# Down products in longer runs: the order of TensorE's work in stage three of a spectral and gated feed-forward kernel

## The chip, the cores and the metric

One core of a Trainium2 chip runs the whole program. The metric is the time on the device in microseconds (us); lower is better. TensorE does the matmuls, VectorE (DVE in the rows) and ScalarE (ACT) read and write the matmuls' results in PSUM, GpSimd (POOL) works on SBUF alone, and SyncE (SP) issues most DMAs. PEld in the rows is TensorE's loading of stationary weights, which runs beside its matmuls.

## The reference, cut to what matters

```python
x = A_x                                              # 2048 x 640
h = x + irfft2(rfft2(layernorm(x)) * (w_r + 1j * w_i))
z = layernorm(h)
return h + ((z @ w_gate) * (z @ w_up)) @ w_down      # 640 -> 1728 -> 640
```

All of it is fp32. The matrices of the last line are larger than in a plain draw (each by a factor of 8), so the products need nearly full fp32 accuracy.

## The kernel before, in words

Stages one and two compute the first line, the two-dimensional transform with its filter. Stage three, from about 165 us on, is the gated feed-forward part, and the change lies there.

Stage three works on two blocks of 1024 tokens. The 1728 hidden features are 13 chunks of 128 and one of 64. Chunks 0 to 11 are taken in pairs p = 0 to 5, an even chunk 2p and an odd one 2p + 1; the rest is handled ahead of them as p = 6. Every matmul operand is split in a high and a low part, so that a product of fp32 numbers is three matmuls (high by high, low by high, high by low).

For each chunk, `strassen` computes gate and up rows of the chunk by seven up products, numbered 1 to 7 here, of 6, 9, 6, 9, 6, 9 and 9 matmuls of 512 columns each (tile `e` in the rows). They go into three PSUM banks: products 1, 3, 5 and 7 are summed in `oa`, products 2 and 4 in `ob`, product 6 in `oc`. In between ACT copies the bank (after 1 to h0, line 1102, after 2 to c22, after 3 to h1), and DVE combines: after product 4 `ob + h1` (line 1122), after 5 two operations (1125, 1126), after 6 `oc + h0` (1132), after 7 the product of gate and up (1147). At the end of an odd chunk DVE and ACT also form and split the operands of the down products (lines 1134 to 1164).

For each pair, the down projection is written to the residual X by down products of 3 matmuls of 320 columns each (tile `d`), each followed by one DVE addition of its PSUM lane to X (line 1047). There are seven kinds, p1 to p7 (`DOWN`, line 1026), by a scheme with sums of operands; each is made for four token blocks j of 128, so 28 per pair. `down_products` writes 14 of them, for two blocks a and b, in the order p1a p5a p1b p5b p6a p3a p6b p3b p7a p2a p7b p2b p4a p4b, and then the same for the two other blocks. Four PSUM banks are the lanes of these products. A lane is taken at p1 and at p5; p6, p7 and p4 are summed on top of p1 of their block in the same lane, p3 on top of p5, and p2 starts afresh in p5's lane. As the lane is added to X after every product, a product may write its lane only after the addition of the product before it in that lane. Fresh lanes are handed out in the order in which they were last read.

The engines' instructions are issued in the order of the code. The down products of one pair are placed between the up products of the next: `strassen` calls `at(n)` behind product n, and `at` issues what `downs` holds for place n, then, in block 1 of two, one or two operations from the queue `fill`, then what `side` holds (splits of weights, loads). `fill` holds the 32 operations of the second block's layer norm statistics (lines 1294, 1295), taken by `pop`. What the five places of the code in `slots` hold is what the change touches; for p = 0 (whose down products are those of the rest, by another function) it is not touched. So five steps in each block have down products of this kind, ten in all, 280 products.

Before, the 28 products lie in ten runs: 3, 3, 3, 2, 3, 3, 3 behind products 1 to 7 of the even chunk, and 3, 2, 3 behind products 2, 3 and 4 of the odd one.

Of the kernel before, what the change touches and what calls it, by code (L numbers as in the profile page):

```python
# [37 lines left out]
SCALE_ON_ACT = (0, *range(AHEAD, NT))  # L38
GROUPS = (((2, 3), (0, 0), (), 1), ((4, 5), (), (0, 0, 1, 1), 3), ((6, 7, 8, 9), (1, 2), (2, 2, 3, 3), 5),
          ((10, 11), (), (4, 5, 6, 7), 9), ((12, 13), (7, 9), (), 11), ((14, 15), (), (8, 9, 10, 11), 13))  # L40
EPS = 1e-5


# [35 lines left out]
def tile_spectral_glu(ctx: ExitStack, tc: tile.TileContext, x, wre, wim, wgu, wlast, wdown, wdlast,  # L79
# [26 lines left out]
    def single():  # L106
        return bank("e", 4)
# [4 lines left out]
    def wk(shape, name):  # L112
        return work.tile(shape, F32, tag="wk", name=name)
# [4 lines left out]
    def mmx(o, l, r, start, stop):  # L118
        nc.tensor.matmul(o, l, r, start=start, stop=stop, skip_group_check=True)  # L119
# [3 lines left out]
    def pop(n=1):  # L123
        for _ in range(n):
            if fill:
                fill.popleft()()
# [38 lines left out]
    def moments(ts, junk=None, total=None, k=0):  # L165
# [4 lines left out]
        def statistics(ts):  # L170
# [11 lines left out]
            fs.append(lambda: nc.vector.tensor_scalar(m2[:, 0:n], mv[:, :, 0], 2.0, None, op0=OP.mult))  # L182
            fs.append(lambda: nc.vector.tensor_scalar(ve[:, 0:n], mv[:, :, 1], EPS, None, op0=OP.add))
            return fs
# [8 lines left out]
        for i, t in list(enumerate(ts))[k:]:  # L193
            if total is None:
                fs.append(lambda t=t, i=i: act(junk[i], X[t], AF.Identity, scale=2.0 / D, accum_out=m2[:, i:i + 1]))
            fs.append(lambda t=t, i=i: act(junk[i], X[t], AF.Square, bias=m2[:, i:i + 1], scale=-2.0,
                                           accum_out=sq[:, i:i + 1]))
        fs.append(lambda: nc.vector.tensor_scalar(ve[:, k:n], sq[:, k:n], 0.25 / D, EPS, op0=OP.mult, op1=OP.add))
        return m2, ve, first + fs
# [14 lines left out]
    def front(ts, k):  # L214
        n = len(ts)
        r = small.tile([P, n], F32, tag="r", name="r")
        junk = [fold[:, o:o + D] for o in (NR * 1026, NR * 1026 + D)]
        m2, ve, fs = moments(ts, junk * 2 if k < n else None, k=k)
        for i, t in enumerate(ts):
            SC[t] = r[:, i:i + 1], m2[:, i:i + 1]  # L220
        return fs, inverse_root(ve, r, n)
# [10 lines left out]
    def even(t):  # L232
        f, j = folded(t)
        fs = [(0.47, lambda: nc.vector.scalar_tensor_tensor(view(f, 0, [[321, 2], [1, 161]]),
                                                     view(XP[t], 0, [[320, 2], [1, 161]]), SC[t][1],
                                                     view(XP[t], 640, [[-320, 2], [-1, 161]]),
                                                     op0=OP.subtract, op1=OP.add))]
        fs.append((0.14, lambda: tt(j[:, 0:64], f[:, 128:192], f[:, 449:513], op=OP.add)))
        fs.append((0.4, lambda: tt(view(j, 64, [[1, 2], [2, 160]]), view(f, 161, [[-161, 2], [1, 160]]),
                                   view(f, 482, [[-161, 2], [1, 160]]), op=OP.subtract)))  # L240
        return fs
# [58 lines left out]
    for ts, when, aside, root in GROUPS:  # L300
        k = len(when)
        fs, cs = front(ts, k)
# [15 lines left out]
    for t in range(NT):  # L318
        if t == 1:
            nc.gpsimd.dma_start(frall, frem)  # L320
        if t >= 1:
            fs = even(t)
# [237 lines left out]
    for g in range(NG - 1):  # L560
# [4 lines left out]
        if g + 3 == NG:  # L565
            xt = home("big", [P, 2, 5, 2, 512], "xt", F32R)
            flat = xt[:, 1].rearrange("p k l n -> p (k l n)")
# [180 lines left out]
    def scale_shift(ts, junk, total=None):  # L748
        n = len(ts)
        r = small.tile([P, n], F32, tag="r", name="r")  # L750
        b = small.tile([P, n], F32, tag="b", name="b")
        m2, ve, fs = moments(ts, junk, total)
        cs = inverse_root(ve, r, n)
        cs.append(lambda: nc.vector.scalar_tensor_tensor(b, m2, -0.5, r, op0=OP.mult, op1=OP.mult))
        for i, t in enumerate(ts):
            SC[t] = r[:, i:i + 1], b[:, i:i + 1]
        return fs, cs
# [108 lines left out]
    for ts in (range(3), range(3, 6), range(6, 8)):  # L866
        n, t0 = len(ts), ts[-1] + 1
        fs, cs = scale_shift(ts, [scrap] * n, total[:, ts[0]:t0])
# [120 lines left out]
    def operand(sb, k):  # L989
        return xt[:, sb, k, 0], xt[:, sb, k, 1]  # L990
# [71 lines left out]
    def hi_of(src, a):  # L1062
        act(hop[:, a, 0], src, AF.Copy)  # L1063

    def lo_of(src, a, engine=nc.vector):
        engine.tensor_tensor(hop[:, a, 1], src, f32(hop[:, a, 0]), op=OP.subtract)  # L1066
# [5 lines left out]
    def strassen(c, blk, ahead, downs, side):  # L1072
        wa, ws = W[c]
        p, odd = divmod(c, 2)

        def at(n):
            if downs.get(n):
                for f in downs[n]:
                    f()
                if c:  # L1080
                    pop(2 if c in (2, 4) else 1)
            for f in side.get(n, ()):
                f()

        b11, b21, b22 = ([operand(sb, k + i) for i in range(2)] for sb, k in ((0, 0), (0, 2), (1, 2)))
        t1, t2 = ([(TJ["12"][:, 0, m, k], TJ["12"][:, 1, m, k]) for k in range(2)] for m in range(2))
        t4 = [operand(1, k) for k in range(2)]
        b5 = [operand(sb, 4) for sb in range(2)]

        def product(o, first, w, a, ms, extra=()):  # L1090
            terms = [(w, a + P * i, m) for i, m in enumerate(ms)] + list(extra)
            n = len(terms)
            for i, (w, a, m) in enumerate(terms):
                whi, wlo = w[:, 0, a:a + P], w[:, 1, a:a + P]
                mmx(o, whi, m[0], first and i == 0, False)
                mmx(o, whi, m[1], False, False)
                mmx(o, wlo, m[0], False, i == n - 1)

        oa = single()
        product(oa, True, wa, 384, b11)  # L1100
        h0 = wk([P, 512], "h0")
        act(h0, oa, AF.Copy)  # L1102
        for f in side.get(0, ()):
            f()
        if ahead and c:
            ahead[0]()
            ahead[1]()
        at(1)
        ob = single()
        product(ob, True, ws, 256, t1, [(wa, 896, b5[1])])  # L1110
        c22 = wk([P, 512], "c22")
        act(c22, ob, AF.Copy)
        if not c:
            ahead[0]()
            ahead[1]()
        at(2)
        product(oa, False, ws, 0, t2)
        h1 = wk([P, 512], "h1")
        act(h1, oa, AF.Copy)  # L1119
        at(3)  # L1120
        product(ob, False, ws, 896, b22, [(ws, 512, b5[1])])
        tt(ob, ob, h1, op=OP.add)  # L1122
        at(4)
        product(oa, False, ws, 640, [(t3[k][:, 0], t3[k][:, 1]) for k in range(2)])
        tt(c22, oa, c22, op=OP.add)
        tt(ob if odd else h1, ob, c22, op=OP.mult)  # L1126
        if odd:
            hi_of(ob, 2 if p < 5 else 4)
        at(5)
        oc = single()  # L1130
        product(oc, True, wa, 0, b21, [(wa, 256, b5[0])])
        tt(h0, oc, h0, op=OP.add)
        if odd and p < 5:
            tt(oc, ob, HELD["a21"], op=OP.add)
            hi_of(oc, 3)
            lo_of(ob, 2)
            tt(ob, ob, HELD["s3"], op=OP.subtract)
            hi_of(ob, 4)
            lo_of(oc, 3)
        elif odd:  # L1140
            lo_of(ob, 4)
        if ahead and not odd:
            ahead[2]()
            ahead[3]()
        at(6)
        product(oa, False, wa, 640, t4, [(wa, 896, b5[0])])
        tt(oa if c == 11 else h0, oa, h0, op=OP.mult)
        if not odd:
            HELD["a11"], HELD["a21"] = h0, h1
            if p < 5:  # L1150
                nc.gpsimd.tensor_tensor(c22, h0, h1, op=OP.subtract)
                HELD["s3"] = c22
        at(7)
        if odd and p < 5:
            hi_of(h0, 1)
            lo_of(ob, 4)
            act(oc, h0, AF.Copy)
            tt(ob, h0, ob, op=OP.subtract)
            hi_of(ob, 6)
            lo_of(oc, 1)  # L1160
            lo_of(ob, 6)
        elif odd:
            hi_of(oa, 5)
            lo_of(oa, 5)
# [5 lines left out]
    for n, (blk, p) in enumerate(steps):  # L1170
        if p == 6:
# [121 lines left out]
            if blk == 0:  # L1293
                fs, cs = scale_shift(range(8, 16), None)
# [5 lines left out]
        slots = [{}, {}]  # L1300
        if prev[1] == 6:
            fs = [[lambda j=j, prev=prev: down(*prev, j)] for j in range(8)]
            slots = [dict(zip(range(4, 8), fs[0:3] + [fs[3] + fs[4]])), dict(zip((2, 3, 4), fs[5:]))]
        else:
            fs = down_products(*prev, (0, 1)) + down_products(*prev, (2, 3))
            slots[0] = dict(zip(range(1, 8), fs))
            slots[1] = dict(zip((2, 3, 4), fs[7:]))
        for ci in range(2):
            c = 2 * p + ci
            side = {n: [] for n in range(8)}  # L1310
# [217 lines left out]
```

## Time and profile before

| what | value |
|---|---|
| median of 3 runs | 675.24 us (674.69 to 675.34) |
| the profiled execution | 674.77 us, of which the span 673.0 |
| TensorE matmuls | 662.0 us busy, 98% of the span |
| VectorE | 471.6 us busy, 70% |
| ScalarE | 322.7 us busy, 48% |
| GpSimd | 393.6 us busy, 58% |

The span runs from the first to the last instruction of the program. The busy shares are averages over stages with different limits. In the chain of waits, what ended last is followed back from the end of the program, at each step to what released it; a piece on that chain counts in full, and work beside it costs nothing as long as it stays beside it. Matmuls overlap in the rows, since each is shown until its result is out: the step from one start to the next is the time that it costs.

### The profile page before, as it was taken

The page shows a single profiled execution, that of the slowest core. Times are in us where ns is not written, and L with a number is a line of the kernel's source. Part 1 is how long each engine was busy: PE and PEld are TensorE (multiplying, and loading weights), DVE is VectorE, ACT ScalarE, POOL GpSimd, SP SyncE. Part 2 cuts the span into 40 slices and gives each one's busy share as a digit, 9 for nine tenths or more (in the row PEclk, how much of TensorE's full clock was granted, in tenths as well). Part 3 has the DMA queues.
Part 4 walks back from the last instruction along what each step waited for, and adds up shares of the span by engine and source line. Part 5 has one row for each costly group of instructions (what it writes and reads, how often), then busy time and mean ns, then how long its engine had stood idle before and what let it go on. Part 6 is the DMA issues. An engine that isn't in the chain of part 4 may idle for free.

```text
span 673.0 us, 10263 instructions
## 1 busy us (share of the span) xinstructions
PE 662.0 (98%) x3695; PEld 587.0 (87%) x3695; DVE 471.6 (70%) x967; ACT 322.7 (48%) x622; POOL 393.6 (58%) x377
## 2 busy tenths in 40 slices
PE   6999999999999999999999999999999999999997
PEld 6999998887898888888888899888888888888887
DVE  6969996788757868594857567754747575756654
ACT  6977774585525244463626246634434252525220
POOL 3101124650297987878787544188787878787610
PEclk9999999999999999999999999999999999999999
DMA  9639884502212110042332458212002121212004
GB/s 317 226 104 283 242 256 142 170 1 79 78 40 78 40 70 23 27 119 59 96 81 79 98 125 265 79 40 76 11 32 79 40 78 40 79 40 80 1 1 156
DMA packets 48953, 66.12 MB, mean 98 GB/s; under 512 B 24082, under 2 KB 30670, under 8 KB 48774
## 3 DMA queue, kind: packets, MB, share of 16 engines
q1 hardware_dynamic: 48246, 62.91, 30.3%
q0 software_dynamic: 288, 2.16, 0.8%
q8 instruction: 29, 0.48, 0.3%
q10 hardware_dynamic: 368, 0.39, 0.3%
q14 instruction: 22, 0.18, 0.1%
HBM read 54.61 MB, written 10.84 MB: 97 GB/s over the span
## 4 chain that ended last, share of the span: by engine, by line
PE 92%; DMA 4%; DVE 2%; ACT 1%; issue 1%; SPq 0%; DVEq 0%; ACTq 0%
PE e L119 49%; PE d L119 26%; PE eo L119 4%; PE re L119 2%; PE u L455 2%; PE y L119 2%; PE im L119 2%; PE im L507 2%; DMA x<-in_x_dram 2%; PE im L252 1%; DMA bits<-in_mm_dram 1%; PE ir L507 1%; DMA wts<-in_wre_dram 1%; PE y L773 0%; ACT xt L783 0%
## 5 line engine op out<-in xcount | busy, mean ns | idle before, releaser
L119 PE MATMUL e<-xt,wst 128*128 128x512 f32 x864 | 213.2, 391 | 0.0
L119 PEld LDWEIGHTS e<-xt,wst 128*128 128x128 f32 x864 | 159.8, 188 | 30.6
L1047 DVE TENSOR_TENSOR x<-d,x 128x320 f32<-128x320 f32 x280 | 123.4, 484 | 51.6 <-PE d L119 47.5
L119 PE MATMUL d<-wd,ht 128*128 128x320 f32 x832 | 143.6, 308 | 0.0
L119 PEld LDWEIGHTS d<-wd,ht 128*128 128x128 f32 x832 | 131.1, 188 | 7.6
L961 POOL TENSOR_TENSOR wst<-raw,wst 128x1024 fp32r<-128x1024 f32 x23 | 55.5, 2412 | 66.9 <-ACT wst L960 49.0
L119 PE MATMUL e<-t,wst 128*128 128x512 f32 x360 | 94.3, 392 | 0.0
L119 PEld LDWEIGHTS e<-t,wst 128*128 128x128 f32 x360 | 66.3, 188 | 12.6
L119 PE MATMUL d<-wt,ht 128*128 128x320 f32 x360 | 69.5, 310 | 0.0
L977 POOL TENSOR_TENSOR wst<-raw,wst 128x896 fp32r<-128x896 f32 (+1 forms) x46 | 65.1, 1439 | 0.2 <-ACT wst L972 0.2
L119 PEld LDWEIGHTS d<-wt,ht 128*128 128x128 f32 x360 | 57.3, 188 | 2.3
L1063 ACT ACTIVATE ht<-e 128x512 fp32r<-128x512 f32 x44 | 26.4, 600 | 51.4 <-DVE e L1126 25.8
L1102 ACT ACTIVATE h<-e 128x512 f32<-128x512 f32 x24 | 14.3, 596 | 67.2 <-PE e L119 67.2
L1022 DVE TENSOR_TENSOR x<-d,x 128x320 f32<-128x320 f32 x62 | 27.5, 485 | 23.2 <-PE d L119 23.2
L658 ACT ACTIVATE wd<-draw 128x320 fp32r<-128x320 f32 (+1 forms) x30 | 15.7, 558 | 57.5 <-POOL draw L668 54.3
L972 ACT ACTIVATE wst<-raw 128x896 fp32r<-128x896 f32 (+1 forms) x48 | 30.2, 676 | 26.8 <-POOL raw L966 26.0
L119 PE MATMUL e<-xt,wdir 128*128 128x512 f32 x180 | 42.0, 392 | 0.4 <-DVE w L207 0.2
L119 PEld LDWEIGHTS e<-xt,wdir 128*128 128x128 f32 x180 | 33.4, 188 | 8.2 <-ACT xt L783 0.7
L1122 DVE TENSOR_TENSOR e<-e,h 128x512 f32<-128x512 f32 x24 | 16.8, 699 | 30.7 <-PE e L119 17.7
L1066 DVE TENSOR_TENSOR ht<-e,ht 128x512 fp32r<-128x512 f32 x54 | 37.0, 685 | 1.6 <-ACT ht L1063 1.3
L637 POOL TENSOR_TENSOR wd<-draw,wd 128x640 fp32r<-128x640 f32 x8 | 12.5, 1576 | 40.5 <-ACT wd L636 40.5
L1119 ACT ACTIVATE h<-e 128x512 f32<-128x512 f32 x24 | 14.4, 599 | 40.1 <-PE e L119 40.1
(234 smaller groups left out, 1189.4 us busy)
## 6 DMA issues: line engine op xcount, KB each, us to landing
raw<-in_wgu_dram SPq DMA_DIRECT2D x24, 640.0 KB
draw<-in_wdown_dram SPq DMA_DIRECT2D x24, 320.0 KB
wts<-in_wre_dram SPq DMA_DIRECT2D x16, 322.0 KB
x<-in_x_dram SPq DMA_DIRECT2D x15, 320.5 KB
out_dram<-x SPq DMA_DIRECT2D x15, 320.0 KB
bits<-in_mm_dram SPq DMA_DIRECT2D x32, 128.0 KB
wts<-in_wim_dram SPq DMA_DIRECT2D x9, 322.0 KB
zfar<-zr SPq DMA_DIRECT2D x32, 80.0 KB
```

Source lines behind the costliest of these rows:

```text
L119: nc.tensor.matmul(o, l, r, start=start, stop=stop, skip_group_check=True)
L507: nc.tensor.matmul(out, y[:, h, a:b], inv(g, h), start=n == 0, stop=n == len(ys) - 1)
L658: act(o[:, 0, a:a + n], src, AF.Copy)
L961: ptt(wa[:, 1], stage[:, 0:1024], f32(wa[:, 0]), op=OP.subtract)
L972: act(ws[:, 0, o:o + b - a], stage[:, a:b], AF.Copy)
L977: ptt(ws[:, 1, o:o + b - a], stage[:, a:b], f32(ws[:, 0, o:o + b - a]), op=OP.subtract)
L1022: tt(xv, ps[b][:, 0:320], xv, op=OP.add)
L1047: tt(xv, o, xv, op=OP.add)
L1063: act(hop[:, a, 0], src, AF.Copy)
L1066: engine.tensor_tensor(hop[:, a, 1], src, f32(hop[:, a, 0]), op=OP.subtract)
L1119: act(h1, oa, AF.Copy)
L1122: tt(ob, ob, h1, op=OP.add)
```

## The change

`RUNS` gives the lengths of five runs. The 28 down products keep their order and are cut into runs of 3, 7 and 7 behind products 1, 3 and 6 of the even chunk and of 6 and 5 behind products 2 and 4 of the odd chunk. The operations in `fill` are now taken at every place of chunks 1 and later (not behind products 6 and 7 of an odd chunk), one at a time and two behind product 3, whether or not down products lie there; before, they were taken only at places with down products, two at a time in chunks 2 and 4.

```diff
+RUNS = (3, 7, 7, 6, 5)
...
         def at(n):
-            if downs.get(n):
-                for f in downs[n]:
-                    f()
-                if c:
-                    pop(2 if c in (2, 4) else 1)
+            for f in downs.get(n, ()):
+                f()
+            if c and not (odd and n > 5):
+                pop(2 if n == 3 else 1)
             for f in side.get(n, ()):
                 f()
...
             fs = down_products(*prev, (0, 1)) + down_products(*prev, (2, 3))
-            slots[0] = dict(zip(range(1, 8), fs))
-            slots[1] = dict(zip((2, 3, 4), fs[7:]))
+            flat, runs = iter(sum(fs, [])), []
+            for n in RUNS:
+                runs.append([next(flat) for _ in range(n)])
+            slots = [dict(zip((1, 3, 6), runs)), dict(zip((2, 4), runs[3:]))]
```

## Rows read from the trace of the kernel before

**Rows 1.** The profile's page: busy time by engine; TensorE's granted clock in 40 slices.

```profile
PE 662.0 (98%) x3695; PEld 587.0 (87%) x3695; DVE 471.6 (70%) x967; ACT 322.7 (48%) x622; POOL 393.6 (58%) x377
...
PEclk9999999999999999999999999999999999999999
```

**Rows 2.** Chain of waits, 309 to 332 us: start us, us, what.

```profile
309.14 3.42 PE e L119 x15
...
319.52 6.83 PE e L119 x30
326.34 1.31 PE d L119 x9
327.66 2.06 PE e L119 x9
329.72 1.35 PE d L119 x9
331.08 1.39 PE e L119 x6
```

**Rows 3.** Busy time by window, two pairs: window, us, engines' busy us (instructions), clock.

```profile
308.98:346.01 37.03, 37.03 (x194) 32.55 (x193) 25.91 (x50) 17.34 (x28) 29.71 (x27) 1.00 0.33 81
...
528.10:565.20 37.10, 37.10 (x195) 32.55 (x194) 23.71 (x47) 14.90 (x25) 29.73 (x27) 1.00 0.16 54
```

**Rows 4.** The profile's page, costliest groups: weight loads of down products, busy, mean ns.

```profile
L119 PEld LDWEIGHTS d<-wd,ht 128*128 128x128 f32 x832 | 131.1, 188 | 7.6
```

**Rows 5.** Chain of waits: the first and the last run of the longer kind.

```profile
255.52 1.42 PE d L119 x9
...
623.04 1.41 PE d L119 x9
```

**Rows 6.** Timeline of DVE, PE and PEld, 329 to 330 us: start, us, instructions.

```profile
329.33 2.07 DVE L1047 TENSOR_TENSOR x<-d,x 128x320 f32<-128x320 f32 x5
329.56 0.60 PE L119 MATMUL d<-wd,ht 128*128 128x320 f32 x3
329.93 0.44 PEld L119 LDWEIGHTS d<-wt,ht 128*128 128x128 f32 x3
```

**Rows 7.** The additions of line 1047: duration ns min/median/max, first and last start.

```profile
L1047 DVE TENSOR_TENSOR x<-d,x x280: 436/481/494, 218.1 to 650.1; 128x320 f32<-128x320 f32 x140
```

**Rows 8.** Timeline of ACT and PE, product 2 of an even chunk.

```profile
291.55 0.59 ACT L1102 ACTIVATE h<-e 128x512 f32<-128x512 f32 x1
...
292.46 0.60 PE L119 MATMUL d<-wd,ht 128*128 128x320 f32 x3
```

**Rows 9.** Timeline of PE and DVE, the run behind product 6 of an even chunk.

```profile
341.32 1.48 PE L119 MATMUL d<-wd,ht 128*128 128x320 f32 x9
341.52 0.69 DVE L1132 TENSOR_TENSOR h<-e,h 128x512 f32<-128x512 f32 x1 [0.77 <-PE e L119]
342.13 1.28 DVE L1047 TENSOR_TENSOR x<-d,x 128x320 f32<-128x320 f32 x3
```

**Rows 10.** Timeline of DVE and PEld, 105 to 106 us, stage two.

```profile
105.29 0.42 DVE L540 TENSOR_TENSOR qr<-ir,qr 64x256 fp32r<-64x256 f32 x1
...
105.76 0.19 PEld L507 LDWEIGHTS ir<-bits,y 128*65 128x65 f32 x2 [0.50 <-DVE qr L540]
```

**Rows 11.** Timeline of PE and DVE, products 4 to 6 of an odd chunk.

```profile
318.04 0.60 PE L119 MATMUL d<-wd,ht 128*128 128x320 f32 x3
318.31 0.70 DVE L1122 TENSOR_TENSOR e<-e,h 128x512 f32<-128x512 f32 x1 [1.64 <-ACT wst L972]
318.92 1.27 DVE L1047 TENSOR_TENSOR x<-d,x 128x320 f32<-128x320 f32 x3
...
321.67 0.70 DVE L1126 TENSOR_TENSOR e<-e,c 128x512 f32<-128x512 f32 x1
322.98 0.69 DVE L1132 TENSOR_TENSOR h<-e,h 128x512 f32<-128x512 f32 x1 [0.61 <-PE e L119]
```

**Rows 12.** Groups of DVE, 180 to 290 us: statistics of block 2; busy, mean ns.

```profile
L176 DVE BATCH_NORM_STATS2 st<-x 128x6 f32<-128x320 f32 x8 | 3.9, 482 | 0.0
L179 DVE BATCH_NORM_STATS2 st<-x 128x6 f32<-128x320 f32 x8 | 3.7, 467 | 0.0
L180 DVE BATCH_NORM_AGGREGATE mv<-st 128x2 f32<-128x12 f32 x8 | 1.6, 198 | 0.0
```

**Rows 13.** Timeline of POOL, start of an even chunk.

```profile
330.20 2.41 POOL L961 TENSOR_TENSOR wst<-raw,wst 128x1024 fp32r<-128x1024 f32 x1 [4.38 <-PE d L119]
```

## The prediction

> **What bounds the kernel now.** I read the busy shares first: TensorE is busy 98% of the 673.0 us span, at full granted clock in every slice [rows 1]. Then the chain of waits: in stage three it consists of nothing but TensorE's two kinds of stretch, up products ("e", 512 columns) and down products ("d", 320 columns), one behind the other [rows 2]. So here a microsecond off any other engine is worth nothing, and only three things count: the matmuls (which stay the same), what a change of stretch costs, and waits inside the stretches. A pair of chunks lasts 37.03 to 37.10 us [rows 3].
>
> The chain gives the steady step. From 15 to 30 up matmuls is 6.83 - 3.42 = 3.41 us, so 0.227 us each; 9 down matmuls take 1.31 us, 0.146 to 0.147 each [rows 2]. A pair has 108 up and 84 down matmuls: 108 x 0.2267 + 84 x 0.1467 = 36.80 us. The pair of 37.03 us thus holds 0.23 us that is no matmul. In it one run of nine down matmuls takes 1.35 us instead of 1.31 [rows 2]; the other 0.19 us is spread over ten places where a down run ends and an up product begins: 0.02 us each (an up stretch of 9 shows it, 2.06 - 9 x 0.227 = 0.02).
>
> **Part 1, fewer runs: -1.0 us.** The change makes ten runs of a pair into five. It concerns the steps whose step before was one of chunks 0 to 9, five in each block, ten in all: 10 x 5 x 0.02 = 1.0 us saved. Number of matmuls, adds and DMAs stays.
>
> For this the Trainium skill has a rule (TensorE: Matmul & The Clock Gate, LDWEIGHTS): a load takes its columns over 1.2 GHz, some 107 ns for 128, which would hide behind a 320-column matmul and leave a change of stretch free. The page of the profile has 188 ns for such a load, longer than the 147 ns step of a down run [rows 4], and the pair's sum leaves 0.02 us. By the rule part 1 would be worth nothing and the sum 1.0 us higher.
>
> **Part 2, the run behind product 2 of the even chunk goes: -0.75 us.** In each of the ten pairs this run is late once: four times it takes 1.35 us, six times 1.41 or 1.42, instead of 1.31 [rows 2, 5], 4 x 0.04 + 6 x 0.10 = 0.76 us. The reason is in the engines' order of time. VectorE comes out of the odd chunk's closing chain late and adds the first three products only from 329.33, 0.48 us each [rows 6, 7], so the first ends at 329.81. Product p6 of the first token block is summed into the same PSUM lane and may not write before that; its weights load at 329.93 [rows 6]. After the change p6 comes one up product (1.39 us) later, when these adds, 0.40 apart, are long done. Nothing is late in its place: products 2 and 3 now follow each other, and product 3 overwrites what ACT copies to h0; that copy ends at 291.55 + 0.59 = 292.14 where product 2 ends at 292.46 [rows 8], and product 3's first load is due a step earlier, at 292.24. It is covered by about 0.05 us; without cover it costs as much as it is late, 0.05 x 10.
>
> **Part 3, the longer runs wait for VectorE: +2.9 us.** Each product is 0.44 us of TensorE and is followed by one VectorE add of 0.48 us, or 0.40 from start to start when they queue [rows 7, 9]. In its token pair product p7 and product p4 of the second token block stand three places apart in the order and share a lane. Before, a long up product lay between them. Now they fall into one run twice per pair: as first and fourth of the run behind product 6 (even), as second and fifth of the run behind product 4 (odd). In front of both runs' adds VectorE still has an operation of the up product.
> - Behind product 6: the run begins at 0; the operation of line 1132 starts at +0.20 and the first add at +0.81 (341.52 and 342.13 against 341.32 [rows 9]), so that add ends at 1.29. The fourth product is due at 1.32 and its weight load one step earlier, at 1.17. A load that waits for one VectorE result starts 0.05 us after it (105.29 + 0.42, then 105.76 [rows 10]), so at 1.34: 0.17 late. In the late run above the load came 0.08 after its due time (329.85, where the third matmul began) and cost 0.04 [rows 6], so 0.04 is slack: 0.13 us lost.
> - Behind product 4: line 1122 starts at +0.27 and the first add at +0.88 (318.31, 318.92 against 318.04 [rows 11]). The second add ends at 0.88 + 0.40 + 0.48 = 1.76; the fifth product's load is due at 4 x 0.44 - 0.15 = 1.61 and can start at 1.81: 0.20 late, 0.16 lost.
> Together 0.29 us per pair, ten pairs: 2.9 us. Queued behind the waiting load are the rest of the run and the next up product; nobody but TensorE waits for these, but TensorE is the chain. The trace has no run of more than three products of this order, so the bounds: if the adds come in time it is 0; if each load answers a result after 0.12 us (329.81 to 329.93 [rows 6], a load with a second semaphore) it is 0.06 more twice, 4.2 us. I take 0.05, since p4 only waits for VectorE.
> The runs of seven behind product 3 and of six behind product 2 (odd) have nothing of VectorE in front, and lanes there come back after four products: the first add starts 0.20 after its product's 0.44, as line 1132 does after its own [rows 9], and ends at 1.12, against a load due at 1.61; the others follow at TensorE's own 0.44. Free.
>
> **Part 4, block 2's layer norm spread: 0.** 32 small operations, of which 16 are statistics of 0.47 to 0.48 us and 8 are of 0.20 [rows 12], some 9 us of VectorE, move to more places. TensorE waits for none now, and they stand behind the adds of their place. One place is new in front of work: behind product 5 of an odd chunk; there VectorE sits idle 0.61 us before line 1132 [rows 11], enough for one. Without that room it would be 0.1 us in two chunks.
>
> Other queues: no DMA is moved on SP or POOL. ACT's split of the down weights waits for the pair's last down product, which stands at the same distance from the next pair; POOL behind it has 4.38 us of idle time [rows 13].
>
> **Sum.** -1.0 - 0.75 + 2.9 = +1.15 us on the profiled execution's 674.77 (673.0 of span), 675.9. The median of the runs, 675.24, lies 0.47 higher: 676.4 us, 0.17% slower. A measurement of this kernel tells about 0.2% from no change, 673.9 to 676.6, so this is "the same", at its upper edge.
>
> **Rivals.**
> - The adds keep up: parts 1 and 2 alone, 675.24 - 1.75 = 673.5 us. For it: VectorE is not the bound, and the waits are computed to within 0.15 us. Against: in [rows 6] TensorE waits on just such an add.
> - Loads answer late, the slower one: if p4's load behind product 6 and behind product 4 carries a second semaphore, it starts 0.12 us after the add. +4.2 in place of +2.9: 677.7 us. It decides for slower once 0.31 us or more are lost per pair. For it: p6's load does so. Against: p4's other inputs are older.
> - Lanes come back in turn: if the first product of the second token pair, fifth in the run behind product 6, takes the lane of p4 two places before it, its load is due at 1.74 and that add ends at 2.08: 0.35 more per pair, 679.9 us. Against: in the program a fresh lane is the one read last longest ago.
> - Changing stretch is free: if the 0.19 us that a pair holds beside its matmuls and its late run [rows 2, 3] belongs to something that stays, part 1 saves nothing, 677.4 us. For it: the chain shows no idle piece at these places. It is what the rule of the Trainium skill above would do here.
> - One of the two waits does not come, 674.8 to 675.1 us.
>
> **Chances.** Forecast 45% (own range 675.6 to 677.0, a fifth of it above 676.6), adds keep up 20%, late loads 17%, lanes in turn 8%, free changes 5%, one wait 5%. Faster by over 0.2%: 0.20. Within: 0.36 + 0.05 = 0.41. Slower: 0.09 + 0.17 + 0.08 + 0.05 = 0.39. The range from 673.4 to 678.6 leaves out lanes in turn and the edges.
>
> **What would show it.** Right: five down stretches per pair in the chain, of 9, 21, 21, 18 and 15 matmuls; the second 21 takes 3.2 instead of 3.08 us with the gap before its tenth matmul, the 15 takes 2.36 instead of 2.20 with the gap before its thirteenth, and no other run is late; a pair lasts 37.2 us. Wrong: no gaps (a pair of 36.9), or a gap before the thirteenth matmul of the second 21.

## The result, and the profile after

| | before | after |
|---|---|---|
| median of 7 runs each, on one chip | 675.01 us (674.69 to 675.34) | 677.23 us (676.90 to 677.43) |
| the profiled execution, its span | 674.77, 673.0 | 677.23, 675.5 |
| VectorE busy | 471.6 us | 476.4 us |

The ratio of the runs is 1.0033, 95% interval 1.0024 to 1.0042: 2.2 us slower, 0.33%. The forecast said +1.15 us. It lies 0.83 us below the measured time, and its own range (675.6 to 677.0) ends just short of it; by the bound of 0.2% the case is "slower", to which 0.39 had been given, and not "the same" with its 0.41.

The page of the changed kernel, busy time by engine and the granted clock (they answer to [rows 1]):

```profile
PE 663.9 (98%) x3695; PEld 587.5 (87%) x3695; DVE 476.4 (71%) x967; ACT 321.3 (48%) x622; POOL 393.1 (58%) x377
...
PEclk9999999999999999999999999999999999999999
```

The number of instructions is the same on each engine, and so is the clock. VectorE has the same 967 operations and is busy 4.8 us longer. 2.0 us of that lie in six operations of block 2's layer norm (lines 183, 184 and 207 to 210, a few numbers each: 2.16 us together before, 4.12 after). They last longer, and more on that is below. Most of the rest is overlap: operations that queue overlap in the rows, and fewer do, so that the durations of all 967 add up to only 2.6 us more.

The chain of waits of the changed kernel over a pair and a little more (start, us, what; it answers to [rows 2]; line 120 is the helper's line 119 of before):

```profile
295.33 3.08 PE d L120 x21
298.40 5.46 PE e L120 x24
303.87 3.20 PE d L120 x21
307.07 5.46 PE e L120 x24
312.53 2.63 PE d L120 x18
315.17 3.42 PE e L120 x15
318.59 2.36 PE d L120 x15
320.96 6.84 PE e L120 x30
327.80 1.31 PE d L120 x9
```

Five down stretches, of 9, 21, 21, 18 and 15 matmuls. The first 21 takes 3.08 us and the second, of the same matmuls, 3.20; the 15 takes 2.36 where 15 x 0.1467 is 2.20. The others are in time. That is the pattern that the prediction wrote down, to the digit. TensorE's timeline of the second 21 shows where its gap is: a row that joins two products' matmuls ends late.

```profile
303.70 0.60 PE L120 MATMUL d<-wt,ht 128*128 128x320 f32 x3
304.14 0.60 PE L120 MATMUL d<-wd,ht 128*128 128x320 f32 x3
304.58 1.17 PE L120 MATMUL d<-wt,ht 128*128 128x320 f32 x6
305.59 0.60 PE L120 MATMUL d<-wd,ht 128*128 128x320 f32 x3
```

From the row of 304.58 to the next row are 1.01 us for six matmuls instead of 0.88: 0.13 us more. VectorE beside it, and the load that waited (PEld), which belongs to the tenth matmul:

```profile
303.90 0.69 DVE L1132 TENSOR_TENSOR h<-e,h 128x512 f32<-128x512 f32 x1 [0.59 <-PE e L120]
304.51 1.76 DVE L1048 TENSOR_TENSOR x<-d,x 128x320 f32<-128x320 f32 x4
```

```profile
305.05 0.19 PEld L120 LDWEIGHTS d<-wt,ht 128*128 128x128 f32 x1
```

Line 1132 starts 0.20 after the stretch (303.70; the chain counts it from 303.87, when the matmul before it is out) and the first add at +0.81, as [rows 9] had it for the shorter run. That add lasts 0.48 us, to 304.99, and the load starts 0.05 us behind it, 0.17 after its due time of 304.88. In the run of 15 the load of the thirteenth matmul is the late one. It is due at 320.04, the second add ends at 320.19, and it starts at 320.24:

```profile
320.24 0.19 PEld L120 LDWEIGHTS d<-wt,ht 128*128 128x128 f32 x1 [0.16 <-DVE x L1048]
```

Busy time by window over one pair of the changed kernel (window, us, busy us of PE, PEld, DVE, ACT and POOL, clock, DMA share, GB/s; it answers to the second line of [rows 3]):

```profile
540.64:577.85 37.21, 37.21 (x195) 32.59 (x194) 23.98 (x47) 14.78 (x25) 29.70 (x27) 1.00 0.15 53
```

This pair takes 37.21 us; 37.2 had been predicted. Before, six of the ten pairs took some 37.10 us and four, those whose run behind product 2 was late by only 0.04, took 37.03 to 37.05. So the ten grow by 0.1 to 0.2 us each, 1.3 us together, and by the traces' starts they are 2.3 us longer: about 0.9 us is not in the pattern. Following the starts of the same up products in both traces, the lag grows evenly by 0.1 to 0.2 us a pair, but by 0.9 us more in one place, the run behind product 6 of chunk 4 in the first block. There the chain of waits leaves TensorE for the only time in these ten pairs:

```profile
265.14 1.69 DVE ve L184
266.83 0.59 DVE h L1132
...
267.87 2.02 PE d L120 x12
```

Line 184 is the addition of EPS to the variances, `ve`, one of the 32 operations of block 2's layer norm that part 4 priced at nothing. It works on 128x8 numbers and lasts 1.69 us. VectorE's and GpSimd's timelines at that place:

```profile
263.07 0.16 DVE L183 TENSOR_SCALAR m<-mv 128x8 f32<-128x8 f32 x1
...
265.14 1.69 DVE L184 TENSOR_SCALAR ve<-mv 128x8 f32<-128x8 f32 x1
266.75 0.68 DVE L1132 TENSOR_TENSOR h<-e,h 128x512 f32<-128x512 f32 x1
267.35 3.08 DVE L1048 TENSOR_TENSOR x<-d,x 128x320 f32<-128x320 f32 x7
```

```profile
264.67 2.13 POOL L978 TENSOR_TENSOR wst<-raw,wst 128x896 fp32r<-128x896 f32 x1
```

Its sister of line 183, with the same shape, takes 0.16 us. Line 184 meets GpSimd's subtraction of line 978, which runs from 264.67 to 266.80; line 184 itself ends at 266.83. Line 1132 and the seven adds stand behind it on VectorE, 0.96 us late (1.16 after the stretch's start of 265.59 instead of 0.20), and the fourth product's load waits for the first of the adds: the stretch takes 265.59 to 269.73, 4.14 us instead of 3.20. So the sum has a term of 0.94 us that the prediction did not have.

### The profile page after: what moved, and what is told of

Its sections match the earlier page's. It is cut to its first block, busy times and chain, and to the rows that moved or that the text cites. A ratio compares the mean times of both kernels' runs of the same rounds, so it can differ in the third digit from the quotient of the medians.

```text
span 675.5 us, 10244 instructions
## 1 busy us (share of the span) xinstructions
PE 663.9 (98%) x3695; PEld 587.5 (87%) x3695; DVE 476.4 (71%) x967; ACT 321.3 (48%) x622; POOL 393.1 (58%) x377
## 3 DMA queue, kind: packets, MB, share of 16 engines
q0 software_dynamic: 288, 2.16, 0.8%
## 4 chain that ended last, share of the span: by engine, by line
PE 92%; DMA 4%; DVE 3%; issue 1%; ACT 1%; SPq 0%; DVEq 0%; ACTq 0%
PE e L120 49%; PE d L120 26%; PE eo L120 4%; PE re L120 2%; PE u L456 2%; PE y L120 2%; PE im L120 2%; PE im L508 2%; DMA x<-in_x_dram 2%; DMA bits<-in_mm_dram 1%; PE im L253 1%; PE ir L508 1%; DMA wts<-in_wre_dram 0%; PE y L774 0%; DVE ve L184 0%
## 5 line engine op out<-in xcount | busy, mean ns | idle before, releaser
L120 PE MATMUL e<-xt,wst 128*128 128x512 f32 x864 | 210.9, 390 | 0.0
L120 PEld LDWEIGHTS d<-wd,ht 128*128 128x128 f32 x832 | 129.7, 188 | 4.4
L120 PE MATMUL d<-wt,ht 128*128 128x320 f32 x360 | 72.2, 315 | 0.8 <-DVE x L1048 0.8
```

## The experiments

Theory: parts 1 to 3 cost what the prediction said, and the rest is this one small operation, held by GpSimd's instruction in flight. Rivals: the spread of the layer norm costs something everywhere; the 1.69 us was a chance of one place; the long runs cost in another way than by the two waits. Each kernel was timed beside the kernel before on the same chip (medians of before 675.05, 675.23, 674.9 and 675.11 in the four sets: runs e1 to e4, e5 to e8, e9 to e11, e12).

### The operation that was held

**e1_runs_alone**: the new runs, with the layer norm's operations taken about where they were before.

```diff
-            if c and not (odd and n > 5):
-                pop(2 if n == 3 else 1)
+            if c in (2, 4):
+                pop(2)
+            elif odd and n in (2, 3, 4):
+                pop(1)
```

> The five longer runs, with the layer norm's operations taken at the places of before. Theory A (a small VectorE operation on SBUF waits until the GpSimd operation in flight has ended; in the changed kernel one such, the eps addition of line 184, took 1.69 us in front of the run behind product 6 of chunk 4): that operation no longer stands there, but at place 5 of chunk 4 now stand two others that took 0.63 and 0.80 us in the kernel before (lines 207, 208), so about half comes back: 676.5 to 676.9 us, the run of 21 in chunk 4 about 3.6 us. Rival B (the long step of 1.1 us belongs to the longer run itself): 677.2, run of 21 still 4.1 us. Rival C (only the spreading costs): 676.2, run of 21 at 3.2 us like its nine siblings.

Measured: 677.54 us, ratio 1.0038 (1.0025 to 1.0050). I had expected it to be 0.3 to 0.7 us faster than the changed kernel. It was not, and the same stretch of chunk 4 was longer still, 265.40 to 270.25, 4.85 us. With two operations taken at a place, two stand in front of line 1134 (1132 of the changed kernel), and each ends with an instruction of GpSimd:

```profile
264.95 1.70 DVE L208 SCALAR_TENSOR_TENSOR w<-r 128x8 f32<-128x8 f32 x1
266.68 0.65 DVE L209 TENSOR_TENSOR w<-w,ve 128x8 f32<-128x8 f32 x1
267.25 0.68 DVE L1134 TENSOR_TENSOR h<-e,h 128x512 f32<-128x512 f32 x1
```

```profile
264.50 2.12 POOL L978 TENSOR_TENSOR wst<-raw,wst 128x896 fp32r<-128x896 f32 x1
...
266.59 0.71 POOL L978 TENSOR_TENSOR wst<-raw,wst 128x256 fp32r<-128x256 f32 x1
```

Line 208 ends at 266.65, 0.03 after GpSimd's first instruction (266.62), line 209 at 267.33, 0.03 after its second (267.30). Without the 1.65 us over 3.20 the run would be at 675.9. So the place in front of line 1132 is what costs, in either arrangement, and the expectation's size for it, some 0.4 us, was too small by a factor of four.

**e2_spread_alone**: the kernel before with the new places of the layer norm alone (the second half of the change, without the runs).

> The ten runs of before, with the layer norm's operations spread as in the change. Theory A: the eps addition is again held in front of product 6's operation, but the run behind it has three products none of which needs a lane just read, so TensorE does not notice: 675.0 us, same as before. Rival C (spreading costs by itself): 675.9 to 676.2 us.

Measured: 675.34 us, ratio 1.0003 (0.9995 to 1.0012), no difference. Here two of the small operations are held as well (line 182 lasts 1.20 us, line 183 0.37), and no stretch of TensorE's beside them is longer: in runs of three no later product needs the adds. The spread costs nothing by itself. By e1 the old places cost too, and more, once the run of seven lies behind product 6.

**e3_eps_on_gpsimd**: the changed kernel with that one operation on GpSimd instead of VectorE.

```diff
-            fs.append(lambda: nc.vector.tensor_scalar(ve[:, 0:n], mv[:, :, 1], EPS, None, op0=OP.add))
+            where = nc.gpsimd if n == 8 else nc.vector
+            fs.append(lambda: where.tensor_scalar(ve[:, 0:n], mv[:, :, 1], EPS, None, op0=OP.add))
```

> The changed kernel, but the eps addition of block 2's layer norm (128x8) is done by GpSimd and not by VectorE. Theory A: the run of 21 behind product 6 of chunk 4 falls from 4.14 to 3.2 us and the time by 0.95 to 676.2 to 676.3 us. Rival D (what is held is not this operation but product 6's operation or the adds, by something else in chunk 4): 677.2 us, run still above 4 us.

Measured: 676.31 us, ratio 1.0017 (1.0008 to 1.0026), 0.92 us less than the changed kernel. The stretch of chunk 4 in its chain of waits:

```profile
265.40 3.20 PE d L120 x21
```

It is like its siblings again: the one operation accounts for the unpredicted term of 0.94 us.

**e6_small_op_at_place_5**: e3 with a spare operation of 128x6 on VectorE in front of line 1132 (1137 here) of each even chunk with down products.

```diff
+            if DOWNED[0] and not odd and n == 5:
+                nc.vector.tensor_scalar(spare, ident[:, 0:6], EPS, None, op0=OP.add)
```

> The changed kernel with the addition of EPS on GpSimd (676.31 in its own run), and one spare tensor_scalar of 128x6 on VectorE in front of the multiplication behind product 5 of each even chunk with down products, ten places; its result is read by nothing. Theory A (a small VectorE operation that meets a running GpSimd instruction ends when that one ends): in the trace without the spare operation eight of the ten places meet GpSimd's 2.13 us subtraction, which ends 0.90 to 1.76 us after the multiplication would start; the multiplication and the adds behind it are late by that, sum 9.2, so 683.5 to 686. Rival B (the 1.69 us of the addition of EPS was a chance of that one place, a small operation costs its 0.15 us, which fits into 0.57 us of idle time): 676.3 to 676.5.

Measured: 683.83 us, ratio 1.0126 (1.0113 to 1.0140), as theory A had it. The spare operation's own times (min, median, max in ns), one of the ten in VectorE's timeline with GpSimd beside it, and TensorE's waits:

```profile
L1086 DVE TENSOR_SCALAR spare<-ident x10: 300/1688/1922, 227.8 to 641.0; 128x6 f32<-128x6 f32 x10
```

```profile
303.96 1.72 DVE L1086 TENSOR_SCALAR spare<-ident 128x6 f32<-128x6 f32 x1
```

```profile
303.52 2.82 POOL L979 TENSOR_TENSOR wst<-raw,wst 128x896 fp32r<-128x896 f32 x2
```

```profile
PE d L120 <- DVE x L1049: 6.7, 8, 1.0
```

In all ten places the operation ended 0.02 to 0.03 us after the GpSimd instruction that ran as it began (the first of the two in the row of 303.52 ended at 305.66, the spare operation at 305.69). In eight of them that was late enough to hold up TensorE, idle for 1.0 us at the most.

**e7_batch_norm_stats_at_place_5**: a batch norm statistic over 128x320 in the same place.

> As the run before it, with a spare batch norm statistic over 128x320 (0.48 us in the traces) in the place of the tensor_scalar. Theory A (statistics are not held by GpSimd, so an operation three times as long costs less than the short one): it fits into the 0.57 us of idle time in front of the multiplication at eight of ten places, and makes block's first pair late by up to 0.4 us, two times: 676.3 to 677.2. Rival B (whatever stands on VectorE at that place is held until GpSimd's instruction ends): 683.5 to 686. Rival C (its time is in front of the adds): 676.3 + 10 x 0.48 = 681.1.

Measured: 676.32 us, ratio 1.0015 (1.0006 to 1.0024), as e3.

```profile
L1086 DVE BATCH_NORM_STATS2 spare<-x x10: 477/483/487, 228.0 to 633.6; 128x6 f32<-128x320 f32 x10
```

GpSimd's same instruction ran beside all ten, and none lasted longer than 0.487 us; in eight places the statistic ended 0.9 to 1.4 us before GpSimd's instruction did. An operation that by itself is three times as long (0.48 us against the 0.16 of line 183) costs 7.5 us less. What matters is the kind of operation, or of its operands, which differ between e6 and e7 too, and not its length.

The Trainium skill (SBUF — State Buffer, Who interferes with whom) says that VectorE and GpSimd share one pair of SBUF ports as an exclusive lock for a whole instruction: a `tensor_scalar` can take it, and a VectorE instruction with two SBUF inputs needs it against a GpSimd instruction that reads SBUF, while one with at most one SBUF input and outside certain modes does not. The traces agree: 1.69 us for the `tensor_scalar` of line 184, 1.70 for line 208 with two inputs, 0.48 for the statistics. That it is this lock no run here shows; the runs show which operations end with GpSimd's.

### The terms of the sum, one by one

**e5_run_behind_2_moved**: the kernel before with the run behind product 2 of the even chunk joined to the one behind product 3, nothing else.

```diff
-            slots[0] = dict(zip(range(1, 8), fs))
+            slots[0] = {1: fs[0], 3: fs[1] + fs[2], 4: fs[3], 5: fs[4], 6: fs[5], 7: fs[6]}
```

> The kernel before with one part of the change alone: the run behind product 2 of the even chunk moves behind product 3, joined to the run that is there; all other runs, the adds and block 2's layer norm stay where they were. Theory A (the run behind product 2 was late for VectorE, 0.04 us in four pairs and 0.10 us in six, and behind product 3 nothing is late; and ten stretches of d less take 20 changes of stretch, 0.01 us each by the prediction's rate, with them): before less 0.75 less 0.2, so 674.1 against 675.05, ratio 0.9986. Rival B (a longer run is late for the adds, as in the changed kernel's run of 21): before plus 0.13 for each of ten pairs less 0.2, 676.1. Rival C (no price for a change of stretch): 674.3.

Measured: 674.33 us, ratio 0.9987 (0.9979 to 0.9996), -0.9 against -0.95 expected by theory A. Busy time by window, one pair:

```profile
545.00:581.98 36.98, 36.98 (x194) 32.55 (x193) 23.77 (x47) 14.89 (x26) 29.65 (x26) 1.00 0.16 56
```

37.10 becomes 36.98: 0.10 for the late run of [rows 5], 0.02 for one run less.

**e9_runs_3_7_7_8_3**: e3 with 8 and 3 in place of 6 and 5 (`RUNS = (3, 7, 7, 8, 3)`), so that p7 and p4 of the second token block no longer share the run behind product 4.

> The changed kernel with the addition of EPS on GpSimd and the odd chunk's runs 8 and 3 in place of 6 and 5, so that p7 and p4 of one token block no longer lie in the run behind product 4; those behind product 6 of the even chunk still do. Theory A (two separate waits, 0.13 us behind product 6 and 0.16 us behind product 4): 676.31 less 10 x 0.16, 674.7, the second run of 21 still 3.20 us. Rival B (one wait that follows from the other, since VectorE's adds come later and later): both go or the one left is the sum of both, 673.4 or 676.3.

Measured: 674.82 us, ratio 0.9999 (0.9990 to 1.0008); theory A's 674.7. In the chain of waits the run behind product 4 is in time, and the second 21 is as it was:

```profile
339.44 3.20 PE d L120 x21
```

**e4_runs_3_8_6_8_3**: e3 with both waits taken away (`RUNS = (3, 8, 6, 8, 3)`).

> As the run with the eps addition on GpSimd, but runs of 3, 8, 6, 8, 3 in the same five places: p7 and p4 of the second token block no longer lie in one run. Lane theory (p4 waits for the add of p7 because that add queues behind an up product's operation): all ten pairs lose 0.13 + 0.16 us of waits, 676.25 - 2.95 = 673.3 us, faster than before by 1.7 us (0.98 for 50 changes of stretch, 0.75 for the late run behind product 2). Rival E (long runs wait whatever their cut): 675.5 us or more, with gaps inside the runs of 8.

Measured: 673.34 us, ratio 0.9973 (0.9962 to 0.9984). It beats both kernels, with five runs in the same five places as the changed kernel; against e3 the runs' ends alone have moved, by one or two products. Windows of one pair, e9 and then e4:

```profile
546.70:583.73 37.03, 37.03 (x194) 32.58 (x193) 23.89 (x47) 14.80 (x27) 29.76 (x26) 1.00 0.16 54
```

```profile
545.97:582.87 36.90, 36.90 (x195) 32.57 (x194) 23.71 (x47) 14.79 (x27) 29.76 (x26) 1.00 0.16 54
```

The wait behind product 6 is 37.03 - 36.90 = 0.13 us, and nine runs against five, both without a late one, are 36.98 - 36.90 = 0.08, 0.02 a run.

### Fewer runs still

**e8_three_runs_13_12_3**: three runs, 13 behind product 3 and 12 and 3 behind products 2 and 4 of the odd chunk.

> The changed kernel with the addition of EPS on GpSimd and the 28 products in three runs: 13 behind product 3 of the even chunk, 12 and 3 behind products 2 and 4 of the odd one, so that products 7 of the first token block and 4 of the second that share a buffer are never in one run's late part. Theory A (each change of stretch costs 0.01 us, two stretches less in each of ten pairs against five runs of 3, 8, 6, 8, 3): 673.34 less 0.4, 672.9. Rival B (no price for a change of stretch, nothing late): 673.3. Rival C (in runs this long the adds fall behind the products, 0.48 us an add against 0.44 us for three products of a run, so a run of 12 is late by up to 0.3 us): 673.3 + 10 x 0.6 = 679.

Measured: 685.0 us, ratio 1.0144 (1.0129 to 1.0160), and no theory of the three was right. Rival C's direction was, its place was not: the runs of 12 and 13 are in time to the last matmul. What is late is an up product, product 2 of the even chunk. Its chain of waits:

```profile
326.15 0.70 DVE h L1133
...
329.43 0.61 DVE h L1148
330.04 0.14 issue
330.18 3.88 PE e L120 x15
```

VectorE's closing operations of the odd chunk run one behind the other from line 1133 on, and the operation of line 1148 ends at 330.04, 0.69 us after TensorE is done with all that lies before product 2 (24 up matmuls from 323.91). The run of three behind product 1 had covered that with its 1.31 us. This wait is not all: a pair of e8 takes some 38.1 us, 1.2 more than one with nothing late. Product 2 starts 0.83 us after its turn, and the other 0.3 to 0.4 us are single steps of products 2 and 3 that take 0.24 to 0.34 us instead of 0.227. What holds those the record does not show; they go with the wait in the next run. The prediction had asked what each run waits for, not what waits behind it.

**e10_runs_3_10_12_3**: that run of three is back, the other long ones stay: 3, 10 | 12, 3.

> The changed kernel with the addition of EPS on GpSimd and four runs: 3 and 10 behind products 1 and 3 of the even chunk, 12 and 3 behind products 2 and 4 of the odd one. Against the three runs 13, 12, 3 (685.0) only the run of three behind product 1 is back. Theory A (the 685.0 came from product 2 of the even chunk, which waited 0.67 us ten times for VectorE's closing operations of the odd chunk; the 1.32 us of the run behind product 1 had covered them): nothing waits, 673.34 less 10 x 0.02, 673.1. Rival B (runs of 10 to 12 are what costs): about 684.

Measured: 672.87 us, ratio 0.9971 (0.9962 to 0.9980), theory A, and nothing is late; a pair has 0.02 us less than with five runs:

```profile
545.42:582.30 36.88, 36.88 (x195) 32.57 (x193) 23.84 (x47) 14.79 (x27) 29.69 (x26) 1.00 0.16 54
```

**e11_runs_3_11_14**: 3, 11 | 14.

> As the run before it with three runs: 3 and 11 behind products 1 and 3 of the even chunk and all 14 of the second token pair behind product 2 of the odd one. Theory A (the run behind product 1 is the only one that covers anything): 673.1 less 10 x 0.02, 672.9. Rival B (the run behind product 4 of the odd chunk covers VectorE's operations behind product 4, so that product 5 waits): up to 0.6 us in each of ten pairs, 679.

Measured: 675.54 us, ratio 1.0010 (1.0001 to 1.0019). Both theories missed. In the chain of waits both long runs are late, here by 0.10 and 0.12 us:

```profile
603.96 6.26 PE d L120 x42
...
625.18 4.96 PE d L120 x33
```

42 x 0.1467 is 6.16 and 33 x 0.1467 is 4.84. In both, p4 of the second token block stands three products behind p7 in the same lane once more. No operation of an up product is in front of these adds. But the adds fall behind in a long run: in the run of 11 the first starts 0.20 us after its product's three steps (625.66) and the eighth, p7's, 0.35 after (628.89). It ends at 629.37 and the load of p4 starts at 629.42, 0.15 after its due time of 629.27. In three pairs of the first block the run of 11 is later still, by 0.20 to 0.28 us; there a transpose of 0.85 us (line 1364) stands in front of its first add. And once more a small operation is held, in front of product 5's additions of chunk 4, where it costs 0.4 us:

```profile
264.53 2.12 DVE L183 TENSOR_SCALAR m<-mv 128x8 f32<-128x8 f32 x1
```

GpSimd's subtraction beside it ends 0.03 us earlier. Ten times 0.22, 0.4 for the transposes and 0.4 here make 3.0 us; the median lies 2.6 above the forecast.

**e12_runs_3_10_14_1**: the run of 14 shifted by one, so that p4 falls to the head of it and to a lone product behind product 4: 3, 10 | 14, 1.

> The changed kernel with the addition of EPS on GpSimd and runs 3 and 10 behind products 1 and 3 of the even chunk, 14 and 1 behind products 2 and 4 of the odd one. The run of 14 holds products 14 to 27 of the 28, so that p4 of the second token block, three places behind p7 of the same block and lane, falls once to the head of the run and once to the lone product behind product 4. Theory A (runs 3, 11, 14 were slow because both their long runs hold such a p7 and p4): nothing waits, as with runs 3, 10, 12, 3, ratio 0.997, 672.9. Rival B (the run of 14 is late for its length, its adds falling behind): 0.10 us a pair, 673.9 or more.

Measured: 672.78 us, ratio 0.9960 (0.9947 to 0.9974), theory A. Its chain of waits has the 42 matmuls in time:

```profile
308.86 6.16 PE d L120 x42
```

So a run of 14 is late with the pair of p7 and p4 in it and in time without; the length alone does not make it late. e10 and e12 beat the kernel before by 2.0 and 2.3 us, and their intervals overlap.

## Why the prediction was right and where not

**Part 1, -1.0: right.** Pairs with nothing late take 36.98, 36.90 and 36.88 us with nine, five and four runs: 0.02 us for each run less, and five less in ten pairs are 1.0. The rival by which a change of stretch is free falls with it. The rule of the Trainium skill (TensorE: Matmul & The Clock Gate, LDWEIGHTS), by which such a load would take an estimated 107 ns, does not hold for these loads of 188 ns. Whether the length of the loads is what a change of stretch costs no run here shows.

**Part 2, -0.75: right.** e5, which does it alone, gains 0.9 us, of which 0.2 are the ten runs less; 0.7 is left.

**Part 3, +2.9: right in place, cause and size.** 0.13 us behind product 6 (e9 against e4) and 0.15 behind product 4 (37.18 us a pair in e3, 37.03 in e9), 2.8 us in ten pairs; with both gone the median falls by 2.97 (e3 to e4). The rivals fall with the same rows: the adds do not keep up, both waits come, the loads answer after 0.05 us (304.99 to 305.05, 320.19 to 320.24) and not after 0.12, and no gap stands in front of the thirteenth matmul of the second 21. The upper bound of this part had a slip: 0.12 instead of 0.05 is 0.07 more twice, which makes 4.3 us, not 0.06 and 4.2. In the first pair of each block line 1132 starts 0.26 us after the stretch instead of 0.20, and the run takes 3.26: 0.1 us in all, whose cause stays open (in the first block a statistic stands in front of line 1132 there, but ends 0.28 us before it; in the second nothing does). That the other two runs are free was right: their lanes come back after four products. Wrong in that clause is that the adds follow at TensorE's own 0.44: in e11 the eighth is 0.15 us behind that, which four products' distance covers and three does not.

**Part 4, 0: wrong, +0.94 us, and with it the sum.** The step that failed is "One place is new in front of work: behind product 5 of an odd chunk". Behind product 5 of an even chunk operations were taken before too, and I took them as priced by that; but now they stand in front of a run whose fourth product waits for the adds, and part 3 itself worked out that line 1132 has no room there. And the price of an operation was read from group means. That such operations are held could have been seen, though not the 1.69 us: the two `tensor_scalar` operations of before took 0.16 and 0.19. The trace of before has two other operations of that shape stretched at that very place, each to GpSimd's end:

```profile
266.58 0.63 DVE L207 SCALAR_TENSOR_TENSOR w<-r 128x8 f32<-128x8 f32 x1
267.24 0.80 DVE L208 TENSOR_TENSOR w<-w,ve 128x8 f32<-128x8 f32 x1
```

Two operations on eight numbers per partition that take 0.63 and 0.80 us are a sign, where others of the shape take 0.16; they end at 267.21 and 268.05, GpSimd's instructions beside them at 267.19 and 268.02. [Rows 12] grouped the statistics, which are not held, and left out the smaller operations, of which `tensor_scalar`, `scalar_tensor_tensor` and `tensor_tensor` are.

**The sum.** -1.0 - 0.75 + 2.8 + 0.1 + 0.94 = +2.1 us; +2.22 was measured between the medians, +2.46 between the profiled executions. The mechanism of the forecast was there; the term left out moved the result from the upper edge of "the same" into "slower".

## What to carry to other kernels

When work is joined into longer runs, list for each step of a run what it needs from the engine beside it and how many steps back that was made (here three was too near and four was enough), and for each gap that the joining closes what that gap had covered; where the runs are cut then counts as much as how many there are (the same five places gave 677.23 us and, with other cuts and one operation moved, 673.34). An operation in front of a chain without room is priced by how long it can be held, here up to a GpSimd instruction of 2.13 us, and not by its mean; the longest row of its shape in the trace (0.80 us before) is a sign and no bound. A tiny operation with a long row that ends with another engine's instruction is held, and harmless only where nobody waits behind it.

## What the runs showed of the hardware

VectorE operations of 128x8 and 128x6 between SBUF tiles (`tensor_scalar`, `scalar_tensor_tensor` and a `tensor_tensor` with two SBUF inputs) lasted 0.16 to 0.18 us where no instruction of GpSimd held them (lines 183 and 210 of the changed kernel, line 208 of e2), and up to 2.12 us where they met a GpSimd subtraction of 2.13 us (1.92 in e6, 2.12 in e11). They ended 0.02 to 0.03 us after GpSimd's instruction, in ten of ten places of e6. Batch norm statistics at the same places lasted 0.48 us. A weight load that waited for a VectorE addition started 0.05 us after its end (304.99 to 305.05 and 320.19 to 320.24 in the changed kernel). I had expected small operations to cost their own time.
